# How the second layer's rows reach their experts: blocks stored by token and gathered by an inverted slot table

## The chip, the cores and the metric

The kernel runs on one core of one Trainium2 chip. The metric is the device time of one execution in microseconds (us). Before the change three runs took 1382.59, 1383.05 and 1385.24 us, median 1383.05.

## The reference

```python
def _moe2_ref(x, w_gate, w1, w2):          # x: 1536 tokens x 512, 8 experts, 192 tokens each
    ...
    for idx in order:                      # (token, expert) pairs by falling logit
        tok, e = (int(idx) // E, int(idx) % E)
        if assigned[tok] >= 0 or counts[e] >= cap:
            continue
        assigned[tok] = e
        counts[e] += 1
    ...
    for e in range(E):
        mask = assigned == e
        h = np.maximum(x[mask] @ w1[e], 0.0)
        out[mask] = h @ w2[e]

def reference(**kwargs):
    attn_out = _attn_ref(**attn_kwargs)    # banded attention with 8 global keys
    x = ...                                # 1536 x 512
    x = _moe_ref(x=x, **moe_kwargs)        # first layer: every token through all 8 experts, weighted
    return _moe2_ref(x=x, **moe2_kwargs)   # second layer: every token through one expert
```

## The kernel before, in words

The program runs attention, the dense first layer, and the routed second layer. A Tile scheduler puts the instructions of each engine in an order; `pin` keeps chosen matmuls as they are written, and `tc.issue_after` holds instructions back behind another one on the same engine.

The output of the first layer, `acc` (12 blocks of 128 tokens by 512, one block a column `c`), is the input of the second. Its last products are *held back* (`held_back`, L823 to L843): they run as filler between the steps of the routing, which is seven rounds of proposals and a last one (L1007 to L1087) on small tables. Blocks are finished in the order 8 to 11, 0 to 3, 4 to 7 (`by_time`, L1113); the last four are added by VectorE (L841), the others by ScalarE and GpSimd (L838, L839).

After the rounds twelve small matmuls (L1092, L1094) and three VectorE operations give every token its *slot* `sf` (L1099): expert e has the slots 192e to 192e+191, so a slot says which row of the second layer's input the token becomes. Then:

- `absmax_bound` (L1115, ScalarE) and `pow2_scale` (L1117, helper L98) give one scale `sx2` for all rows. `pow2_scale` reduces over the partitions on GpSimd when the list `on_pool` is filled, otherwise with a matmul by `ident` (L105) and VectorE (L106).
- Twelve indirect stores on GpSimd (L1122) scatter the blocks to the DRAM tensor `xg` by slot. The rows have 513 columns: the last holds the token's number (L1119).
- `load_rows(a)` (L1157) loads the 384 rows of a pair of experts from `xg` with four direct loads on SyncE's queue (L1161 to L1164) into `xr`, three blocks of 128 rows. `turn_rows(a)` (L1168) transposes them on TensorE (L1175), splits them into two f16 parts (L1177, L1178) and copies the token numbers out (L1180).
- For each of four pairs TensorE makes the first product (`mm3`, L710 to L712, by `split_relu` at L1213) and the second (L1224, L1234); `scatter` (L1129, indirect stores on GpSimd at L1130) puts each result at its token's row of `out`.

The second layer's weights lie in DRAM as sixteen `ws` tensors of 2 MB; `fetch` (L1147) loads one into a slot that earlier work has left, from SyncE's queue (L1151). A queue issues in its own order: a load that waits holds back what stands behind it. Before the change the loads of the sixth and seventh weights stand behind the rows of pairs 0 and 1:

```python
    fetch_next(5)
    load_rows(0)
    st = load_rows(1)
    turn_rows(0)
    with tc.issue_after(st.ins):
        fetch_next(2)
```

The slot of the sixth weights held the first layer's W2 of expert 6, which the last held-back product still reads.

Of the kernel before, what the change touches and what calls it, by code (L numbers as in the profile page):

```python
# [20 lines left out]
P = 128  # L21
# [19 lines left out]
def tile_sparse_attention_moe_moe(ctx, tc, q, k, v, ng, nl, wg1, w11, w12, wg2, w21, w22, out, taps=None):  # L41
# [748 lines left out]
        hidden(*x, steps=1)  # L790
    hidden(0, NTB - 1, steps=1)
    done.add(("hidden", 0))
    acc = lat.tile([P, NC, DM + 1], F32, name="acc", tag="acc", bufs=1)
    L = lat.tile([P, NC, E], F32)
    pfs = {}

# [8 lines left out]
    def expert_out(e, tb, steps=0):  # L805
        h = hs.pop((e, tb))
        w, _ = W[e, 1]
        pf = pfs[e]
        for t in range(CPB):
            c = tb * CPB + t  # L810
            ps = mmbank([P, DM], name="py")
            mm3(ps, lambda z, f: h[:, z, f, t * P:t * P + P], lambda z, f: w[:, z, f, :], FC)
            if e == 0:
                latest["dve"] = nc.vector.tensor_scalar(acc[:, c, :DM], ps, pf[:, c:c + 1], None, op0=ALU.mult)
            else:
                latest["dve"] = nc.vector.scalar_tensor_tensor(acc[:, c, :DM], ps, pf[:, c:c + 1], acc[:, c, :DM],  # L816
                                                               op0=ALU.mult, op1=ALU.add)
            if steps:
                pump(steps)
# [3 lines left out]
    def held_back(e, tb, by_pool):  # L823
# [4 lines left out]
        for t in range(CPB):  # L828
            c = tb * CPB + t
            ps = mmbank([P, DM], name="py")  # L830
            for f in range(FC):
                for n, (y1, y2) in enumerate(((0, 0), (0, 1), (1, 0))):
                    pin(nc.tensor.matmul(ps, h[:, y1, f, t * P:t * P + P], w[:, y2, f, :],  # L833
                                         start=f == 0 and n == 0, stop=f == FC - 1 and n == 2))
                if f == FC - 1:
                    if by_pool:
                        y = rawp.tile([P, TB], F32, name="relu", bufs=3)
                        nc.scalar.activation(y[:, :DM], ps, AF.Copy, scale=pf[:, c:c + 1])  # L838
                        nc.gpsimd.tensor_tensor(acc[:, c, :DM], acc[:, c, :DM], y[:, :DM], op=ALU.add)  # L839
                    else:  # L840
                        nc.vector.scalar_tensor_tensor(acc[:, c, :DM], ps, pf[:, c:c + 1], acc[:, c, :DM],  # L841
                                                       op0=ALU.mult, op1=ALU.add)
                yield  # L843

# [9 lines left out]
    def partial_logits(tb):  # L854

        for c in range(tb * CPB, tb * CPB + CPB):
            am = sml.tile([P, 1], F32, name="gam")
            absmax_bound(acc[:, c, :DM], am, rsm)
# [148 lines left out]
    for rnd in range(E - 1):  # L1007
# [76 lines left out]
        nc.vector.tensor_tensor(b, bc_e(tok), bc_c(T[:, 2]), op=ALU.is_gt)  # L1084
        nc.vector.scalar_tensor_tensor(a, b, 1e-37, a, op0=ALU.mult, op1=ALU.is_gt)
        nc.vector.scalar_tensor_tensor(L, a, -1.0e30, L, op0=ALU.mult, op1=ALU.add)
    propose()  # L1087
    run(2)

# [8 lines left out]
    sf = rsm.tile([P, NC], F32, name="sf")  # L1098
    nc.vector.tensor_reduce(sf, sl, axis=AX.X, op=ALU.add)  # L1099
    nc.vector.tensor_scalar(sf, sf, 0.0, float(NT - 1), op0=ALU.max, op1=ALU.min)  # L1100
    si = lcs.tile([P, NC], I32)
    nc.vector.tensor_copy(si, sf)
    finish(held)
    if "slot" in taps:
        nc.sync.dma_start(taps["slot"].rearrange("(c p) -> p c", p=P), si)

    if "x2" in taps:
        for c in range(NC):
            nc.sync.dma_start(taps["x2"][c * P:(c + 1) * P, :], acc[:, c, :DM])


    xam = rsm.tile([P, NC + 1], F32, name="xam")
    by_time = [x for tb in (2, 0, 1) for x in range(tb * CPB, tb * CPB + CPB)]  # L1113
    for c in by_time:
        absmax_bound(acc[:, c, :DM], xam[:, c:c + 1], rsm)  # L1115
    nc.vector.tensor_reduce(xam[:, NC:], xam[:, :NC], axis=AX.X, op=ALU.max)
    sx2 = pow2_scale(xam[:, NC:], "sx2")  # L1117
    xg = drp.tile([NT, DM + 1], F32)
    nc.gpsimd.iota(acc.bitcast(I32)[:, :, DM:], pattern=[[P, NC]], base=0, channel_multiplier=1)  # L1119
    scs = []  # L1120
    for c in by_time:
        st = nc.gpsimd.indirect_dma_start(out=xg, out_offset=bass.IndirectOffsetOnAxis(ap=si[:, c:c + 1], axis=0),  # L1122
                                          in_=acc[:, c, :], in_offset=None)
        for o in scs:
            tc.declare_no_dep(st.ins, o.ins, reason="slots of other tokens")
        scs.append(st)
    outs = []

    def scatter(o, idx):  # L1129
# [38 lines left out]
    def turn_rows(a):  # L1168
        xr = XR.pop(a)
        idx = rsm.tile([P, 3], I32, name="idx", bufs=E // 2)  # L1170
        x2 = xtp.tile([P, 2, KC, 3 * P], F16, name="xt")
        for kc in range(KC):
            pt = aux([P, 3, P], name="px2")
            for z in range(3):
# [92 lines left out]
```

## Time and profile before

| | |
|---|---|
| median of three runs | 1383.05 us |
| the profiled execution's own time | 1383.23 us |
| its span | 1381.4 us |
| TensorE busy | 1305.9 us (95%) |
| VectorE busy | 816.1 us (59%) |
| ScalarE busy | 596.4 us (43%) |
| GpSimd busy | 162.6 us (12%) |

The engines are PE (TensorE), PEld (its weight loads), DVE (VectorE), ACT (ScalarE), POOL (GpSimd) and SP (SyncE, which only issues transfers). The share of busy time is an average over stages with different limits; the second layer fills the last 170 us of the span, and what the change touches lies between about 1207 and 1245 us.

### The profile page before, as it was taken

How to read it: one execution, taken by the hardware profiler on the slowest of the kernel's cores; microseconds unless marked ns; L12 is line 12 of the kernel's file. 1: busy time of each engine (PE TensorE's matmuls, PEld its weight loads, DVE VectorE, ACT ScalarE, POOL GpSimd, SP SyncE). 2: the span in 40 equal slices, each digit the busy share in tenths (PEclk: the TensorE clock that was granted, in tenths of full speed). 3: DMA queues.
4: the chain of work that ended last, by engine and by line, in shares of the span. 5: the costliest groups of instructions: out<-in, count | busy, mean ns of one | idle time of the engine just before them, and what ended most of it. 6: DMA issues, size and time to landing. Idle time of an engine off the chain costs nothing. (4 is left out here: it accounts for less than half of the span.)

```text
span 1381.4 us, 19879 instructions
## 1 busy us (share of the span) xinstructions
PE 1305.9 (95%) x7956; PEld 671.6 (49%) x7956; DVE 816.1 (59%) x1765; ACT 596.4 (43%) x1053; POOL 162.6 (12%) x259
## 2 busy tenths in 40 slices
PE   5899999999999999999999999999988999919998
PEld 3655544444444444444444444455544444407775
DVE  5787586666666666665665654466537878702121
ACT  3667541344253435324341632456534657403332
POOL 5233210000000000000000000010001434030000
PEclk8999999999999999999999999999998999959999
DMA  8352013526433624451462351130010223148740
GB/s 217 82 150 74 1 61 122 183 71 217 140 123 122 217 88 156 149 183 61 147 202 78 117 188 61 51 132 2 1 61 1 104 81 122 62 143 301 274 199 28
DMA packets 96748, 164.93 MB, mean 119 GB/s; under 512 B 50064, under 2 KB 50064, under 8 KB 94096
## 3 DMA queue, kind: packets, MB, share of 16 engines
q1 hardware_dynamic: 94448, 153.18, 33.3%
q0 software_dynamic: 2208, 10.49, 2.0%
q8 instruction: 62, 1.02, 0.3%
q14 instruction: 30, 0.25, 0.1%
HBM read 119.61 MB, written 44.05 MB: 118 GB/s over the span
## 5 line engine op out<-in xcount | busy, mean ns | idle before, releaser
L710 PE MATMUL ph<-xt,wslot 128*128 128x512 f16 x768 | 291.1, 379 | 0.1
L711 PE MATMUL ph<-xt,wslot 128*128 128x512 f16 x768 | 291.0, 379 | 0.0
L712 PE MATMUL ph<-xt,wslot 128*128 128x512 f16 x768 | 291.0, 379 | 0.0
L703 ACT ACTIVATE hslot<-ph 128x512 f16<-128x512 f32 x192 | 114.1, 594 | 253.7 <-PE ph L712 252.0
L710 PE MATMUL py<-wslot,hslot 128*128 128x512 f16 x576 | 218.3, 379 | 0.0
L711 PE MATMUL py<-wslot,hslot 128*128 128x512 f16 x576 | 218.3, 379 | 0.0
L712 PE MATMUL py<-wslot,hslot 128*128 128x512 f16 x576 | 218.3, 379 | 0.0
L705 DVE TENSOR_TENSOR hslot<-relu,hslot 128x512 f16<-128x512 f32 x192 | 132.2, 689 | 111.2 <-ACT relu L704 110.9
L665 DVE TENSOR_REDUCE wam<-raw 128x1 f32<-128x1024 f32 x120 | 143.9, 1212 | 29.8 <-DMA raw<-in_moe_w_dram 29.7
L618 ACT ACTIVATE spill<-raw,s 128x1024 f16<-128x1024 f32 x64 | 72.6, 1146 | 162.7 <-DVE inv L669 64.7
L833 PE MATMUL py<-wslot,hslot 128*128 128x512 f16 x576 | 132.1, 381 | 0.0
L704 ACT ACTIVATE relu<-ph 128x512 f32<-128x512 f32 (+1 forms) x224 | 129.3, 577 | 0.0
L712 PEld LDWEIGHTS <-wslot 128*128 128x128 f16 x768 | 75.1, 98 | 87.4
L710 PEld LDWEIGHTS <-wslot 128*128 128x128 f16 x768 | 75.1, 98 | 86.9 <-issue 2.4
L711 PEld LDWEIGHTS <-wslot 128*128 128x128 f16 x768 | 75.1, 98 | 85.3
L619 DVE SCALAR_TENSOR_TENSOR spill<-raw,s,spill 128x1024 f16<-128x1024 f32 x64 | 81.9, 1283 | 56.5 <-ACT spill L618 55.3
L618 ACT ACTIVATE wslot<-raw,s 128x1024 f16<-128x1024 f32 (+1 forms) x72 | 73.2, 1050 | 76.0 <-DVE s L114 76.0
L816 DVE SCALAR_TENSOR_TENSOR acc<-py,pf,acc 128x512 f32<-128x512 f32 x60 | 45.0, 750 | 84.8 <-PE py L712 84.8
L710 PEld LDWEIGHTS <-hslot 128*128 128x128 f16 x576 | 56.3, 98 | 68.0
L712 PEld LDWEIGHTS <-hslot 128*128 128x128 f16 x576 | 56.3, 98 | 68.0
L711 PEld LDWEIGHTS <-hslot 128*128 128x128 f16 x576 | 56.3, 98 | 67.9
L619 DVE SCALAR_TENSOR_TENSOR wslot<-raw,s,wslot 128x1024 f16<-128x1024 f32 (+1 forms) x72 | 82.8, 1160 | 10.9 <-ACT wslot L618 10.1
(249 smaller groups left out, 1677.3 us busy)
## 6 DMA issues: line engine op xcount, KB each, us to landing
raw<-in_moe_w_dram SPq DMA_DIRECT2D x64, 1024.0 KB, 6.6
ws<-spill SPq DMA_DIRECT2D x64, 512.0 KB, 3.1
w2slot<-ws SPq DMA_DIRECT2D x16, 2048.0 KB, 9.7
hd<-hslot POOLq DMA_DIRECT2D x2, 2048.0 KB, 6.9
hslot<-hd SPq DMA_DIRECT2D x2, 2048.0 KB
qb<-in_q_dram SPq DMA_DIRECT2D x12, 256.0 KB, 3.4
kb<-in_k_dram SPq DMA_DIRECT2D x12, 256.0 KB, 6.7
vo<-in_v_dram SPq DMA_DIRECT2D x12, 256.0 KB, 3.3
```

The lines of the kernel that those rows point to most:

```text
L618: nc.scalar.activation(hi, raw, AF.Copy, scale=s[:, 0:1])
L619: nc.vector.scalar_tensor_tensor(lo, raw, s[:, 0:1], hi, op0=ALU.mult, op1=ALU.subtract)
L665: nc.vector.tensor_reduce(am[:, a:a + 1], part, axis=AX.X, op=ALU.max, apply_absolute_value=True)
L703: nc.scalar.activation(hi, ps, AF.Relu, scale=HS)
L704: latest["act"] = nc.scalar.activation(r[:, :n], ps, AF.Relu, scale=HS)
L705: latest["dve"] = nc.vector.tensor_sub(lo, r[:, :n], hi)
L710: nc.tensor.matmul(out_, lhs(0, a), rhs(0, a), start=a == 0, stop=False)
L711: nc.tensor.matmul(out_, lhs(0, a), rhs(1, a), start=False, stop=False)
L712: nc.tensor.matmul(out_, lhs(1, a), rhs(0, a), start=False, stop=a == n - 1)
L816: latest["dve"] = nc.vector.scalar_tensor_tensor(acc[:, c, :DM], ps, pf[:, c:c + 1], acc[:, c, :DM], op0=ALU.mult, op1=ALU.add)
L833: pin(nc.tensor.matmul(ps, h[:, y1, f, t * P:t * P + P], w[:, y2, f, :], start=f == 0 and n == 0, stop=f == FC - 1 and n == 2))
```

## The change

Blocks are stored to `xg` by token, not by slot, with twelve direct stores on SyncE's queue. The slots are *inverted* on the chip: with slot s = 128a + p of token t, a table `onep` (token by p) and a table `onea` (token by a, holding the token's number where it is 1) are multiplied block by block on TensorE, which leaves at (p, a) the token that has slot 128a + p. That table, `inv`, is the index of three indirect loads a pair on GpSimd, and of the output scatters. The column with the token's number, its copies and the four direct loads a pair go. `on_pool` is emptied ahead of the scale, so its reduction is done by TensorE and VectorE.

```diff
-    acc = lat.tile([P, NC, DM + 1], F32, name="acc", tag="acc", bufs=1)
+    acc = lat.tile([P, NC, DM], F32, name="acc", tag="acc", bufs=1)
...
+    tabs = rawp.tile([P, NT], F32, name="raw", bufs=2)
+    ramp, cols, sq = tabs[:, :P], tabs[:, P:P + NC], tabs[:, 2 * P:2 * P + NC * NC].rearrange("p (c a) -> p c a", a=NC)
+    nc.gpsimd.iota(ramp, pattern=[[1, P]], base=0, channel_multiplier=0, allow_small_or_imprecise_dtypes=True)
+    nc.gpsimd.iota(cols, pattern=[[P, NC]], base=0, channel_multiplier=0, allow_small_or_imprecise_dtypes=True)
     propose()
     run(2)
...
     si = lcs.tile([P, NC], I32)
     nc.vector.tensor_copy(si, sf)
+    nc.vector.tensor_scalar(si, si, P - 1, None, op0=ALU.bitwise_and)
+    sp = rsm.tile([P, NC], F32, name="sp2")
+    nc.vector.tensor_copy(sp, si)
+    onea = tabs.bitcast(F16)[:, NT:NT + NC * NC].rearrange("p (c a) -> p c a", a=NC)
+    onep = rawp.tile([P, NC, P], F16, name="spill", bufs=2)
+    h6 = NC // 2
+    nc.vector.tensor_tensor(onep[:, :h6], sp[:, :h6, None].to_broadcast([P, h6, P]),
+                            ramp[:, None, :].to_broadcast([P, h6, P]), op=ALU.is_equal)
+    nc.gpsimd.tensor_tensor(sf, sf, sp, op=ALU.subtract)
+    nc.vector.tensor_tensor(sq, sf[:, :, None].to_broadcast([P, NC, NC]),
+                            cols[:, None, :].to_broadcast([P, NC, NC]), op=ALU.is_equal)
+    nc.vector.tensor_tensor(onea, sq, tok[:, :, None].to_broadcast([P, NC, NC]), op=ALU.mult)
+    nc.vector.tensor_tensor(onep[:, h6:], sp[:, h6:, None].to_broadcast([P, h6, P]),
+                            ramp[:, None, :].to_broadcast([P, h6, P]), op=ALU.is_equal)
+    run(0)
+    pi = misc([P, NC], name="pinv")
+    for c in range(NC):
+        pin(nc.tensor.matmul(pi, onep[:, c, :], onea[:, c, :], start=c == 0, stop=c == NC - 1))
+    inv = lcs.tile([P, NC], I32)
+    nc.vector.tensor_scalar(inv, pi, 0.0, float(NT - 1), op0=ALU.max, op1=ALU.min)
     finish(held)
...
+    on_pool.clear()
     sx2 = pow2_scale(xam[:, NC:], "sx2")
-    xg = drp.tile([NT, DM + 1], F32)
-    nc.gpsimd.iota(acc.bitcast(I32)[:, :, DM:], pattern=[[P, NC]], base=0, channel_multiplier=1)
-    scs = []
+    xg = drp.tile([NT, DM], F32)
     for c in by_time:
-        st = nc.gpsimd.indirect_dma_start(out=xg, out_offset=bass.IndirectOffsetOnAxis(ap=si[:, c:c + 1], axis=0),
-                                          in_=acc[:, c, :], in_offset=None)
...
+        nc.sync.dma_start(xg[c * P:c * P + P, :], acc[:, c, :])
...
-        xr = rawp.tile([P, 3, DM + 1], F32, name="raw", bufs=2)
-        r0, r1 = 2 * a * CAP, (2 * a + 1) * CAP
-        nc.sync.dma_start(xr[:, 0, :], xg[r0:r0 + P, :])
-        nc.sync.dma_start(xr[0:RM, 1, :], xg[r0 + P:r0 + CAP, :])
-        nc.sync.dma_start(xr[64:64 + RM, 1, :], xg[r1 + P:r1 + CAP, :])
-        st = nc.sync.dma_start(xr[:, 2, :], xg[r1:r1 + P, :])
+        xr = rawp.tile([P, 3, DM], F32, name="raw", bufs=2)
+        for z in range(3):
+            st = nc.gpsimd.indirect_dma_start(out=xr[:, z, :], out_offset=None, in_=xg,
+                                              in_offset=bass.IndirectOffsetOnAxis(ap=inv[:, 3 * a + z:3 * a + z + 1],
+                                                                                  axis=0))
...
-        nc.vector.tensor_copy(idx, xr.bitcast(I32)[:, :, DM])
-        X2[a] = x2, idx
+        X2[a] = x2, inv[:, 3 * a:3 * a + 3]
```

Where the instructions come to stand is decided by the scheduler. The first place is VectorE behind the sum of the slots. The rows with a + are new, those with a - are of before; L841 is the last block's accumulation.

```order
+L1104 TENSOR_SCALAR sf<-sf 128x12
+L1107 CAST si<-sf 128x12
+L1108 TENSOR_SCALAR si<-si 128x12
+L1110 CAST sp_11066<-si 128x12
+L1114 TENSOR_TENSOR spill<-sp_11066,raw 128x768
+L1117 TENSOR_TENSOR raw<-sf,raw 128x144
+L1120 TENSOR_TENSOR spill<-sp_11066,raw 128x768
+L1119 TENSOR_TENSOR raw<-raw,tok 128x144
+L1127 TENSOR_SCALAR inv<-pinv 128x12
 L841 SCALAR_TENSOR_TENSOR acc<-py,pf,acc 128x512
-L1100 TENSOR_SCALAR sf<-sf 128x12
-L1102 CAST si<-sf 128x12
```

The last accumulation stood ahead of the slots' last two operations and now stands behind the whole inversion. At the same place TensorE now has, between the slots' matmul (L1098) and the scale's (L105), the twelve pairs of L1125 ahead of the last three pairs of L833; before, the L833 pairs followed L1094 directly.

```order
L1098 LDWEIGHTS before
L1098 MATMUL pk<-Bz,before 128x96
L1125 LDWEIGHTS spill [waits DVE_49]
L1125 MATMUL pinv<-raw,spill 128x12 [waits PE_49]
...
L833 LDWEIGHTS hslot
L833 MATMUL py<-wslot,hslot 128x512
...
L105 MATMUL bc<-ident,xam 128x128 [waits DVE_49]
```

So the last held-back product, which the accumulation L841 and the slot of the sixth weights wait for, ends behind matmuls that wait for VectorE.

The second place is SyncE's queue, now, from the second of the second layer's weights on (`ws_1_3898` is the sixth, `ws_0_4070` the seventh; L1143 are the stores).

```order
L1168 DMA w2slot<-ws_1_2559 128x8192
L1143 DMA xg<-acc 128x512 x3
L1168 DMA w2slot<-ws_0_3078 128x8192
L1143 DMA xg<-acc 128x512
L1168 DMA w2slot<-ws_1_3225 128x8192
L1143 DMA xg<-acc 128x512 x3
L1168 DMA w2slot<-ws_0_3413 128x8192
L1143 DMA xg<-acc 128x512 x4
L1168 DMA w2slot<-ws_1_3898 128x8192
L1143 DMA xg<-acc 128x512
L1168 DMA w2slot<-ws_0_4070 128x8192
```

Before, it was:

```order
L1151 DMA w2slot<-ws_0_3413 128x8192
L1161 DMA raw<-xg 128x513
L1162 DMA raw<-xg 64x513
L1163 DMA raw<-xg 64x513
L1164 DMA raw<-xg 128x513
...
L1151 DMA w2slot<-ws_1_3898 128x8192
L1151 DMA w2slot<-ws_0_4070 128x8192
```

The sixth weights stood behind the rows of two pairs; now they stand ahead of the last store, and the seventh directly behind it.

The third place is GpSimd from the last slots to the end.

```order
-L1122 DMA xg<-acc,si 1536x513
-L102 ISA
-L102 ISA amax<-xam 128x1
-L1122 DMA xg<-acc,si 1536x513 x11
-L1130 DMA out_dram<-spill,idx 1536x512 x12
-L1260 UNCONDITIONAL_BRANCH
+L1116 TENSOR_TENSOR sf<-sf,sp_11066 128x12
+L1178 DMA raw<-xg,inv 128x512 x12
+L1147 DMA out_dram<-spill,inv 1536x512 x12
```

Twelve scatters with a reduction among them became twelve gathers, and all twelve stand ahead of the first output scatter.

## Rows read from the trace of the kernel before

**Rows 1.** Head of the page.
```profile
span 1381.4 us, 19879 instructions
```
**Rows 2.** Busy time by stretches: us, each engine (count), granted clock, DMA share, GB/s.
```profile
1238.80:1244.30 5.50, 4.73 (x23) 3.59 (x24) 1.94 (x5) 2.10 (x4) 0.00 (x0) 0.50 0.99 327
1244.30:1300.00 55.70, 55.52 (x523) 43.32 (x521) 14.25 (x28) 21.18 (x45) 2.87 (x3) 1.00 0.87 333
```
**Rows 3.** Timeline at the slots' end: start, us, engine, line, operation, [idle before <-releaser].
```profile
1207.81 0.81 PE L833 MATMUL py<-wslot,hslot 128*128 128x512 f16 x3
...
1208.60 0.25 DVE L1099 TENSOR_REDUCE sf<-sl 128x12 f32<-128x96 f32 x1
1208.77 0.74 DVE L841 SCALAR_TENSOR_TENSOR acc<-py,pf,acc 128x512 f32<-128x512 f32 x1
...
1209.62 0.17 DVE L1102 CAST si<-sf 128x12 int32<-128x12 f32 x1
```
**Rows 4.** Timeline of GpSimd from 1210 to 1232 us.
```profile
1210.10 1.20 POOL L1122 DMA_INDIRECT xg<-acc,si  x1 [24.55 <-DVE si L1102]
...
1217.95 0.38 POOL L102 PARTITION_ALL_REDUCE amax<-xam  x1 [6.65 <-issue]
...
1218.52 1.20 POOL L1122 DMA_INDIRECT xg<-acc,si  x1 [0.20 <-issue]
...
1220.02 0.96 POOL L1122 DMA_INDIRECT xg<-acc,si  x1 [0.30 <-issue]
...
1231.40 0.96 POOL L1122 DMA_INDIRECT xg<-acc,si  x1 [0.30 <-issue]
```
**Rows 5.** Timeline at the restart of TensorE.
```profile
1238.86 0.90 PE L1175 MATMUL px<-ident,raw 128*128 128x128 f32 x3 [30.24 <-DMA raw<-xg]
...
1240.92 0.17 DVE L1180 COPY idx<-raw 128x3 int32<-128x3 int32 x1 [21.89 <-DMA raw<-xg]
...
1241.99 0.80 PE L710 MATMUL ph<-xt,w2slot 128*128 128x192 f16 x4 [0.24 <-ACT xt L1177]
```
**Rows 6.** VectorE's prices: timeline (1181, 1247 us), and the page's costliest groups.
```profile
1180.87 0.17 DVE L1079 TENSOR_SCALAR rtau<-prs 128x8 f32<-128x8 f32 x1 [0.85 <-PE prs L1075]
1181.07 0.16 DVE L1080 TENSOR_TENSOR rtau<-rtau,prs 128x8 f32<-128x8 f32 x1
...
1247.47 0.56 DVE L705 TENSOR_TENSOR xt<-relu,xt 128x384 f16<-128x384 f32 x1 [2.58 <-ACT relu L704]
...
L705 DVE TENSOR_TENSOR hslot<-relu,hslot 128x512 f16<-128x512 f32 x192 | 132.2, 689 | 111.2 <-ACT relu L704 110.9
```
**Rows 7.** Timeline: an addition on GpSimd, and twelve small matmuls.
```profile
1143.22 7.21 POOL L839 TENSOR_TENSOR acc<-acc,relu 128x512 f32<-128x512 f32 x1 [3.98 <-ACT relu L838]
...
1178.10 0.64 PE L1065 MATMUL prc<-comb,spill 128*128 128x8 f16 x12
```
**Rows 8.** SyncE's queue: landing after 1181.45, the issues, landings after 1259.5 and 1262.55, one stretch.
```profile
w2slot<-ws SPq DMA_DIRECT2D x1, 2048.0 KB, 8.8
...
1251.67 8.24 SPq L1151 DMA_DIRECT2D w2slot<-ws  x2
...
w2slot<-ws SPq DMA_DIRECT2D x1, 2048.0 KB, 10.6
...
1262.59 0.99 SPq L1162 DMA_DIRECT2D raw<-xg  x1
...
raw<-xg SPq DMA_DIRECT2D x1, 128.2 KB, 8.6
...
1131.00:1133.00 2.00, 2.00 (x22) 1.08 (x20) 0.70 (x3) 0.44 (x1) 0.00 (x0) 1.00 0.99 426
```
**Rows 9.** Output scatters' landings after 1376 and 1278.5 us, and weight loads' issue.
```profile
out_dram<-spill,idx POOLq DMA_INDIRECT x1, 2.7
...
1276.80 0.80 SPq L1151 DMA_DIRECT2D w2slot<-ws  x2
...
out_dram<-spill,idx POOLq DMA_INDIRECT x1, 8.2
```

More of the change, by code (lines that the diff above doesn't have):

```diff
@@ L813, in expert_out @@
             if e == 0:
-                latest["dve"] = nc.vector.tensor_scalar(acc[:, c, :DM], ps, pf[:, c:c + 1], None, op0=ALU.mult)
+                latest["dve"] = nc.vector.tensor_scalar(acc[:, c, :], ps, pf[:, c:c + 1], None, op0=ALU.mult)
             else:
-                latest["dve"] = nc.vector.scalar_tensor_tensor(acc[:, c, :DM], ps, pf[:, c:c + 1], acc[:, c, :DM],
+                latest["dve"] = nc.vector.scalar_tensor_tensor(acc[:, c, :], ps, pf[:, c:c + 1], acc[:, c, :],
                                                                op0=ALU.mult, op1=ALU.add)
@@ L838, in held_back @@
                         nc.scalar.activation(y[:, :DM], ps, AF.Copy, scale=pf[:, c:c + 1])
-                        nc.gpsimd.tensor_tensor(acc[:, c, :DM], acc[:, c, :DM], y[:, :DM], op=ALU.add)
+                        nc.gpsimd.tensor_tensor(acc[:, c, :], acc[:, c, :], y[:, :DM], op=ALU.add)
                     else:
-                        nc.vector.scalar_tensor_tensor(acc[:, c, :DM], ps, pf[:, c:c + 1], acc[:, c, :DM],
+                        nc.vector.scalar_tensor_tensor(acc[:, c, :], ps, pf[:, c:c + 1], acc[:, c, :],
                                                        op0=ALU.mult, op1=ALU.add)
@@ L857, in partial_logits @@
             am = sml.tile([P, 1], F32, name="gam")
-            absmax_bound(acc[:, c, :DM], am, rsm)
+            absmax_bound(acc[:, c, :], am, rsm)
             s = pow2_scale(am, "sp", bufs=2)
@@ L1102, in tile_sparse_attention_moe_moe @@
     nc.vector.tensor_copy(si, sf)
+    nc.vector.tensor_scalar(si, si, P - 1, None, op0=ALU.bitwise_and)
[18 more added lines that the diff above has]
+    nc.vector.tensor_scalar(inv, pi, 0.0, float(NT - 1), op0=ALU.max, op1=ALU.min)
     finish(held)
-    if "slot" in taps:
-        nc.sync.dma_start(taps["slot"].rearrange("(c p) -> p c", p=P), si)
     if "x2" in taps:
         for c in range(NC):
-            nc.sync.dma_start(taps["x2"][c * P:(c + 1) * P, :], acc[:, c, :DM])
+            nc.sync.dma_start(taps["x2"][c * P:(c + 1) * P, :], acc[:, c, :])
     xam = rsm.tile([P, NC + 1], F32, name="xam")
@@ L1114, in tile_sparse_attention_moe_moe @@
     for c in by_time:
-        absmax_bound(acc[:, c, :DM], xam[:, c:c + 1], rsm)
+        absmax_bound(acc[:, c, :], xam[:, c:c + 1], rsm)
     nc.vector.tensor_reduce(xam[:, NC:], xam[:, :NC], axis=AX.X, op=ALU.max)
+    on_pool.clear()
     sx2 = pow2_scale(xam[:, NC:], "sx2")
-    xg = drp.tile([NT, DM + 1], F32)
-    nc.gpsimd.iota(acc.bitcast(I32)[:, :, DM:], pattern=[[P, NC]], base=0, channel_multiplier=1)
-    scs = []
+    xg = drp.tile([NT, DM], F32)
     for c in by_time:
-        st = nc.gpsimd.indirect_dma_start(out=xg, out_offset=bass.IndirectOffsetOnAxis(ap=si[:, c:c + 1], axis=0),
-                                          in_=acc[:, c, :], in_offset=None)
-        for o in scs:
-            tc.declare_no_dep(st.ins, o.ins, reason="slots of other tokens")
-        scs.append(st)
+        nc.sync.dma_start(xg[c * P:c * P + P, :], acc[:, c, :])
     outs = []
@@ L1169, in turn_rows @@
         xr = XR.pop(a)
-        idx = rsm.tile([P, 3], I32, name="idx", bufs=E // 2)
         x2 = xtp.tile([P, 2, KC, 3 * P], F16, name="xt")
```

## The prediction

> **What bounds the kernel now.** I read the page first: the profiled execution spans 1381.4 us [rows 1] and took 1383.23 us, 1.8 us around the span and 0.18 above the median of the three runs (1383.05), so the sum below is made against 1383.23. Then TensorE's busy time by stretches [rows 2]: from 1244.3 on it is busy 55.5 of 55.7 us, so the second layer is bound by TensorE once it runs. Ahead of it lies a hole: the first transpose at 1238.86 had TensorE idle for 30.24 us, released by the loads of the rows [rows 5]. What the change can win lies there, and the timeline shows what fills it [rows 3 to 5]. The slots are ready at 1209.79 (cast at 1209.62, 0.17 long). The first scatter starts at 1210.10, then GpSimd sits 6.65 us before the reduction for the scale, and eleven scatters follow, one about every 1.27 us, the last starting at 1231.40. Only when all have landed may the rows be loaded back. The copy of the token numbers, which reads all three blocks of the pair, is released at 1240.92, so that is when the pair's last rows are there. The first product starts at 1241.99.
>
> **The sum: when do the last rows of pair 0 land after the change?** Everything behind that moment is TensorE's own work and moves with it.
>
> 1. *Slots to one-hot tables (VectorE).* The sum of slots ends at 1208.85 (1208.60 + 0.25) [rows 3]. Four operations on 12 columns follow each other; two such stand 0.20 us apart [rows 6]: 0.8, to 1209.65. Two compares of 768 elements come next: TENSOR_TENSOR takes 0.56 for 384 and 0.689 for 512 [rows 6], so 0.129 for each 128 more, and 0.95 for 768 (an estimate; the low end is 0.69, the 512 row itself, the high end twice 0.95 if the broadcast operands slow it). Two operations on 144 elements by the same slope take 0.32. Together 2.54, to 1212.2. GpSimd's subtraction of 12 columns runs beside the first compare.
> 2. *Inversion (TensorE).* Twelve matmuls of 12 columns: the twelve of 8 columns took 0.64 at most [rows 7], to 1212.8. The new order puts the last three matmuls of the held-back product behind these; they took 0.81 [rows 3], to 1213.6. The conversion to whole numbers is 0.17 beside them.
> 3. *Last block of x2.* VectorE's accumulation (0.74) [rows 3] therefore ends at 1214.4 and no longer at 1209.51. This is what the inversion costs: 4.9 us.
> 4. *Its store.* In SyncE's queue the last store stands behind a load of 2 MB second-layer weights, whose slot is released by those same three matmuls. So the load leaves at 1213.6 and the store at 1214.5. A load of that size issued at 1181.51 alone landed after 8.8 us [rows 8]: 1222.4. What happens to a small transfer behind a large one also has a row: the second weight load of the 1251.67 piece starts at 1259.59 (the piece's end less one issue of 0.32) and landed 10.6 later, at 1270.2; the 128 KB of L1162 issued behind it at 1262.59 landed 8.6 later, at 1271.2, 1.0 us after it [rows 8]. So the store lands at 1223.4. The other eleven stores are issued as their blocks are done, under TensorE's work, and cost nothing; the cover is that work, and without it each would be one transfer of 256 KB. The weights queued behind them are wanted only after the first product of pair 0.
> 5. *Gathers (GpSimd).* The first starts 0.3 after its last wait, as the first scatter did (1209.79 to 1210.10) [rows 3, 4]: 1223.7. Scatter starts stand 1.50 and then 1.27 apart [rows 4]; the trace has no gather, but it is the same instruction with the direction turned, so the third starts at 1226.5.
> 6. *Landing.* No row shows a gather's. Its low end is a scatter of the same size with nothing beside it, 2.7; its high end one beside two weight loads, 8.2 [rows 9]. I take 4.0, nearer the low end: the weight load queued behind the last store moves 2.1 MB at the 426 GB/s of such a load's middle [rows 8], 4.9 us, so it has most of its data across when the third gather starts, even counted from the store's landing. The last rows land at 1230.5, against 1240.9: **10.4 us earlier**.
>
> Nothing of this comes back later. The scale is not waited for: its reduction ended 8.8 us after the last accumulation (1209.51 to 1218.33), with the 6.65 us in it [rows 3, 4], and 1214.4 + 8.8 is still before 1230.5. The nine gathers of the other pairs stand ahead of the first output scatter in GpSimd's queue; the last three wait for the transposes of pair 1, which come with the end of pair 0's first product, and take 3.8 us, while the first output follows a whole second product later. The removed loads and copies of token numbers were off the path. 1383.23 - 10.4 = **1372.8 us**.
>
> *TensorE's clock.* It was granted 0.50 (1.2 GHz) for the first 5.5 us after the hole and 1.00 (2.4 GHz) after [rows 2]. The new hole is shorter but still over ten us, so I leave the restart as it was. Bounds: those 5.5 us at the full level would give back at most 2.7; transposes that come one block at a time could keep it low 2.8 us longer, which costs 1.4. With the compares (0.5 less to 1.9 more) and the landing (2.7 to 5.3 alone) the forecast's own range is 1370 to 1376.
>
> **The rivals.**
>
> *A: the store overtakes.* If the last store does not wait behind the 2 MB load, it lands 2.7 after 1214.5, at 1217.2, and the third gather starts at 1220.3. Beside two weight loads it lands after 4.0 to 8.2, at 1224.3 to 1228.5: 12.4 to 16.6 us won, 1366.6 to 1370.8. Against it stands L1162's 8.6 us [rows 8]; for it, that this was a load behind a load and not a store.
>
> *B: the gathers are held by the weights.* In the old order the row loads stood ahead of the next weights in one queue; now two weight loads go first and the gathers come from another queue. If the second of them is still streaming, the row is 8.2 us beside loads (two issued from 1276.80, the scatter at 1278.54) against 2.7 alone [rows 9]: the third gather lands at 1234.7, 6.2 us are won, **1377.0**. Against it: by my sum the load's data ends about when the gathers start. The Trainium skill, "DMA: Bandwidth & Descriptors", section "Issuing engines are not separate DMA queues", speaks for this rival: DMAs run on the same 16 engines and interleave whichever engine started them, so issuing the rows from GpSimd gets them past nothing. By that rule, the trace agrees: 8.2 against 2.7 us. The same page's section "Queues, rings and completion order" says that an engine goes round-robin between queues packet by packet, which would cost a 256 KB gather about its own data time again, an estimate of 0.6 us at the page's 436 GB/s; the row of 8.2 is far above that, and the row decides.
>
> *C: the index chain is slow.* GpSimd's subtraction stands between VectorE's operations. An addition on GpSimd beside a busy VectorE took 7.21 us [rows 7]. If this one does too, it outlasts the compare's 0.95 by 6.3 and the gain shrinks to 4.1, 1379.1; with B as well it is no change. Against it: VectorE then waits for it and is no longer in its way.
>
> *D, slower: gathers that don't spread.* The sum lets a gather move its rows over all 16 engines. The scatters did: eleven of 263 KB started within the 12.9 us from 1218.52 to 1231.40 [rows 4], 224 GB/s, or 14 for each engine. If the three gathers of a pair ran through one engine, 786 KB at 14 GB/s are 56 us: rows at 1280 in place of 1240.9, at least 39 us slower, **1422**. It decides from the point at which the third lands after 1240.9, 14.4 us after its start, or under 54 GB/s for the three. Nothing in the trace speaks for it except that it holds no gather.
>
> *E: the change doesn't take effect,* because something other than rows releases the first transposes. The row at 1238.86 names the loads, so I give it next to nothing.
>
> **How the numbers follow.** Forecast 0.57, A 0.13, B 0.19, C 0.06 (half of it within 2.8 us of before), D 0.04, E 0.01. 0.2% is 2.8 us, about what a measurement of this kernel can tell from no change. Faster by more: forecast, A, B and half of C, 0.92, of which I keep 0.91. Within it: half of C and E, rounded to 0.05. Slower: 0.04. The time is the forecast's, 1372.8. The range reaches from the upper part of A (1367.5) over B with a little more (1378.0), and leaves out the lower part of A, C and D.
>
> **What would show it.** Right: GpSimd has no reduction and no 6.65 us wait after 1208; the last store is issued near 1214.5 and the first gather near 1223.7; the first transposes start near 1228 and the first product near 1231.6, with the clock at 0.50 for some 5 us; behind that TensorE is busy without gaps. Wrong: a first gather near 1218 (A); a third gather that takes over 6 us to land while a weight load streams (B); VectorE waiting for GpSimd between the compares (C); gathers that take over 14 us each (D); gaps on TensorE after the restart that end with a transfer.

## The result and the profile after

The changed kernel took 1372.8 us (median; 1371.69 to 1373.88), the kernel before 1384.07 us beside it: ratio 0.9919, 95% interval 0.9902 to 0.9936, some 9 to 13.5 us faster. The profiled execution took 1372.69 us. The forecast was 1372.8.

Where the time went is read best from one point that both kernels pass: the start of the last product that counts places for the slots (`pk`, L1094 before, L1098 after). It stood at 1207.77 before and at 1208.25 after; this start differs by up to 3.7 us between executions of the kernels below, so differences are taken from it and called the **lag**. The first product of the second layer came 34.22 us behind it before (1241.99 [rows 5]) and 23.25 us after. From the same point to the span's end it is 173.63 us before (1381.4 [rows 1]) and 162.65 after: 10.98 us won, of which the lag has 10.97. Nothing was won or lost elsewhere.

The head of the page after:

```profile
span 1370.9 us, 19908 instructions
```

The timeline of VectorE, GpSimd, TensorE and SyncE's queue after, from the slots to the first product (start, length, engine, line, operation, [idle before <- what ended it]; it answers to [rows 3 to 5]):

```profile
1208.25 0.20 PE L1098 MATMUL pk<-Bz,before 128*128 128x96 bf16 x1
1209.08 0.25 DVE L1103 TENSOR_REDUCE sf<-sl 128x12 f32<-128x96 f32 x1
...
1210.20 0.96 DVE L1114 TENSOR_TENSOR spill<-sp,raw 128x768 f16<-128x768 f32 x1
1210.24 0.98 POOL L1116 TENSOR_TENSOR sf<-sf,sp 128x12 f32<-128x12 f32 x1 [24.22 <-DVE sp L1110]
...
1212.35 0.30 DVE L1119 TENSOR_TENSOR raw<-raw,tok 128x144 f16<-128x144 f32 x1
1212.71 0.46 PE L1125 MATMUL pinv<-raw,spill 128*128 128x12 f16 x12 [4.26 <-DVE raw L1119]
1213.03 1.11 PE L833 MATMUL py<-wslot,hslot 128*128 128x512 f16 x3
...
1214.17 0.32 SPq L1168 DMA_DIRECT2D w2slot<-ws  x1
1214.18 0.75 DVE L841 SCALAR_TENSOR_TENSOR acc<-py,pf,acc 128x512 f32<-128x512 f32 x1 [0.80 <-PE py L833]
1214.96 0.32 SPq L1143 DMA_DIRECT2D xg<-acc  x1
...
1217.29 0.22 DVE L1155 TENSOR_SCALAR f<-f,sx 128x8 f32<-128x8 f32 x1
...
1223.84 1.19 POOL L1178 DMA_INDIRECT raw<-xg,inv  x1 [12.61 <-issue]
1225.33 0.95 POOL L1178 DMA_INDIRECT raw<-xg,inv  x1 [0.30 <-issue]
1226.58 0.95 POOL L1178 DMA_INDIRECT raw<-xg,inv  x1 [0.30 <-issue]
...
1228.33 1.70 PE L1190 MATMUL px<-ident,raw 128*128 128x128 f32 x6 [11.85 <-DMA raw<-xg,inv]
1230.36 0.90 PE L1190 MATMUL px<-ident,raw 128*128 128x128 f32 x3 [0.33 <-DMA raw<-xg,inv]
1231.50 0.80 PE L710 MATMUL ph<-xt,w2slot 128*128 128x192 f16 x4 [0.24 <-ACT xt L1192]
```

The reader is to see three waits in a row. VectorE and TensorE make the index until 1213.4, and the last block of x2 is held back behind that (L833 at 1213.03; before, it stood at 1207.81 [rows 3]). The store leaves at 1214.96, behind a load of weights. Then nothing happens on GpSimd until 1223.84: the profile writes "issue" there, since it sees no releaser, but the scale was ready at 1217.5 and the index at 1213.4, so only the store is left to wait for, 8.9 us after its issue (experiments 3 and 4 bear this out). The third gather starts at 1226.58 and its transposes at 1230.36, 3.8 us later.

Busy time by stretches after (us, each engine's busy time (count), granted clock, DMA share, GB/s; it answers to [rows 2]):

```profile
1228.30:1231.50 3.20, 2.60 (x10) 1.64 (x10) 0.02 (x1) 0.63 (x2) 2.38 (x3) 0.50 0.74 210
1231.50:1233.90 2.40, 2.40 (x14) 2.03 (x14) 1.84 (x4) 1.47 (x3) 0.57 (x1) 0.51 0.53 172
1233.90:1289.60 55.70, 55.52 (x523) 43.24 (x522) 13.84 (x25) 21.31 (x45) 8.09 (x9) 1.00 0.70 268
```

The restart is that of before, moved: 2.4 us after the first product the granted clock goes from 0.50 (1.2 GHz) to 1.00 (2.4 GHz), and TensorE is then busy 55.52 of 55.7 us, to the hundredth what [rows 2] has.

### The profile page after: what moved, and what is told of

It reads as the page before. It is cut to its first block, busy times and chain, and to the rows that moved or that the text cites. A ratio compares the mean times of both kernels' runs of the same rounds, so it can differ in the third digit from the quotient of the medians.

```text
span 1370.9 us, 19908 instructions
## 1 busy us (share of the span) xinstructions
PE 1308.3 (95%) x7969; PEld 672.8 (49%) x7969; DVE 819.8 (60%) x1769; ACT 596.5 (44%) x1053; POOL 166.9 (12%) x260
## 4 chain that ended last, share of the span: by engine, by line
PE 78%; issue 10%; DVE 7%; POOL 3%; DMA 1%; ACT 1%; POOLq 0%; SPq 0%; DVEq 0%; ACTq 0%
PE ph L710 12%; PE ph L712 12%; PE ph L711 12%; PE py L710 9%; PE py L712 9%; PE py L711 9%; PE py L833 4%; PE pa L510 2%; PE pe L491 1%; DVE xt L1045 1%; PE ps L465 1%; POOL ex L481 1%; DVE xt L1043 1%; PE pg L138 1%; DVE xt L1046 1%
## 5 line engine op out<-in xcount | busy, mean ns | idle before, releaser
L833 PE MATMUL py<-wslot,hslot 128*128 128x512 f16 x576 | 132.3, 381 | 0.0
L102 POOL PARTITION_ALL_REDUCE amax<-wam x30 | 10.6, 353 | 661.3 <-DVE wam L666 661.3
```

## The experiments

The theory was that of the prediction: the time is set by slots, inversion, last block, store behind a 2 MB load, gathers. All times stand beside the kernel before, run between them (medians 1384.07 to 1385.12 us). The last three columns come from the one profiled execution of each kernel.

| run | time, us | ratio to before, 95% | lag, us | full clock after first product, us | to the end, us |
|---|---|---|---|---|---|
| before | 1384.07 | | 34.22 | 2.5 | 173.63 |
| after | 1372.8 | 0.9919 (0.9902 to 0.9936) | 23.25 | 2.4 | 162.65 |
| after again | 1372.0 | 0.9904 (0.9885 to 0.9922) | 23.57 | 2.1 | 162.86 |
| 1: scale alone | 1376.38 | 0.9947 (0.9931 to 0.9964) | 27.74 | 2.1 | 166.96 |
| 2: scale back on GpSimd | 1374.44 | 0.9926 (0.9909 to 0.9942) | 22.66 | 3.4 | 162.58 |
| 3: store first | 1371.96 | 0.9909 (0.9892 to 0.9926) | 22.67 | 3.2 | 162.44 |
| 4: weights last | 1367.05 | 0.9876 (0.9859 to 0.9892) | 17.66 | 4.2 | 158.00 |
| 5: product first | 1368.55 | 0.9878 (0.9860 to 0.9895) | 18.58 | 3.9 | 158.61 |
| 6: both 4 and 5 | 1364.55 | 0.9849 (0.9831 to 0.9866) | 14.01 | 4.8 | 154.61 |
| 7: other queue | 1374.99 (one run) | | 25.75 | 3.3 | 165.47 |
| 7 again | 1375.95 | 0.9943 (0.9927 to 0.9960) | 25.37 | 3.9 | 165.31 |
| 8: other queue, one load | 1372.41 | 0.9912 (0.9895 to 0.9929) | 23.36 | 5.5 | 164.08 |
| 9: store first, 2 KB pieces | 1371.79 | 0.9905 (0.9888 to 0.9921) | 21.86 | 3.9 | 161.97 |
| 10: other queue, 2 KB pieces | 1372.95 | 0.9914 (0.9896 to 0.9933) | 22.55 | 3.3 | 162.24 |

"To the end" is the span less the start of the last `pk` product. "Full clock" is the start of the first product of the second layer that takes 0.25 us in place of 0.37, less the start of the first product.

### The scale's reduction (1 and 2)

Experiment 1 is the kernel before with one line of the change: the scale's maximum over the partitions goes to TensorE and VectorE.

```diff
+    on_pool.clear()
     sx2 = pow2_scale(xam[:, NC:], "sx2")
```

> The kernel before, with the change's smallest part alone: the scale is reduced by TensorE and VectorE and no longer on GpSimd between the scatters. Theory (the hole is a chain on GpSimd, and its 6.65 us idle piece before the reduction lies on it): the second scatter starts about 1.5 us after the first, near 1211.6 and not at 1218.52, everything behind moves 6.9 us forward, 1376.3 us; so two thirds of the change's gain come from this one line. Rival (the piece is covered, the scatters are paced by their transfers and the gain belongs to the gathers): within 1 us of before.

Measured: 1376.38 us. GpSimd's timeline in experiment 1:

```profile
1208.77 1.20 POOL L1123 DMA_INDIRECT xg<-acc,si  x1 [24.55 <-DVE si L1102]
1210.27 0.96 POOL L1123 DMA_INDIRECT xg<-acc,si  x1 [0.30 <-issue]
...
1222.91 0.96 POOL L1123 DMA_INDIRECT xg<-acc,si  x1 [0.30 <-issue]
```

The first and second scatter stand 1.50 apart where they stood 8.42 apart (1210.10 and 1218.52 [rows 4]); the last starts 14.14 after the first and no longer 21.30. The lag falls from 34.22 to 27.74. So **6.5 of the 11 us of the change belong to this line**, and 4.5 to stores by token and gathers together. The medians would give the line more, 8.3 of 11.3 us, but its profiled execution reached the last `pk` product 1.33 us earlier than that of before, ahead of all that the line touches.

Experiment 2 is the changed kernel without that line.

```diff
-    on_pool.clear()
     sx2 = pow2_scale(xam[:, NC:], "sx2")
```

> The changed kernel with the scale's reduction put back on GpSimd. Theory (GpSimd only waits for the last store at that time): the reduction and the 6.65 us before it end by 1223.5, the first gather still starts near 1223.8, time as after the change, 1372.8 within 1. Rival (the 6.65 us stand in the way as they did between the scatters): the first gather starts 5 us later or more, 1378 or above.

GpSimd's timeline in experiment 2:

```profile
1218.90 0.38 POOL L102 PARTITION_ALL_REDUCE amax<-xam  x1 [5.81 <-issue]
1225.39 1.19 POOL L1177 DMA_INDIRECT raw<-xg,inv  x1 [6.12 <-issue]
```

The reduction comes back, with 5.81 us of idle ahead of it, and costs nothing: it is over at 1219.28, and the gather waits until 1225.39 for the store that left at 1216.52, 8.9 us as in the changed kernel. The lag is 22.66, not longer than 23.25. The time is 1.6 us higher than that of the change, though the two ratios to before can't be told apart (0.9926 and 0.9919, with intervals that overlap); in the profiled executions it lies ahead of the reduction, since this one reached the last `pk` product at 1210.12 and took 162.58 from there to the end, against 162.65. The line is worth 6.5 us in the old order, where GpSimd is the path, and nothing in the new one, where a transfer is.

### The store and the weights (3 and 4)

Experiment 3 issues the two loads of weights behind the last store.

```diff
-        nc.sync.dma_start(xg[c * P:c * P + P, :], acc[:, c, :])
+        last = nc.sync.dma_start(xg[c * P:c * P + P, :], acc[:, c, :])
...
-    st = load_rows(1)
+    load_rows(1)
...
-    with tc.issue_after(st.ins):
+    with tc.issue_after(last.ins):
         fetch_next(2)
```

> The changed kernel with the sixth and seventh weights' loads held behind the last store in SyncE's queue. Theory (the last store lands 8.5 us after its issue because it stands behind 2 MB in the queue): it lands 2 to 3.1 us after its issue at 1215, the first gather starts near 1218.3 (5.5 earlier), the third near 1221; but now both weight loads stream beside the gathers, which land after 4.4 to 8.2 us, so the first product starts between 1226.5 and 1230.4 and the time is 1368 to 1372. Rival (the store shares the engines with the weights whatever the order): it lands near 1222 as before, time within 1.5 of 1372.8.

Measured: 1371.96 us. The timeline in experiment 3, and under it the DMA issues of the first three gathers there (count, median us from issue to landing):

```profile
1213.89 0.32 SPq L1143 DMA_DIRECT2D xg<-acc  x1
1214.30 0.89 SPq L1168 DMA_DIRECT2D w2slot<-ws  x2
...
1217.06 1.19 POOL L1178 DMA_INDIRECT raw<-xg,inv  x1 [6.74 <-DVE f L1155]
...
1225.80 0.90 PE L1190 MATMUL px<-ident,raw 128*128 128x128 f32 x3 [10.39 <-DMA raw<-xg,inv]
1228.25 1.54 PE L1190 MATMUL px<-ident,raw 128*128 128x128 f32 x6 [1.55 <-DMA raw<-xg,inv]
```

```profile
raw<-xg,inv POOLq DMA_INDIRECT x3, 9.0
```

The first gather follows the store's issue by 3.2 us in place of 8.9. (The profile names VectorE's `f` as what released it, as it does in experiment 4; `f` is the operation that ended last, at 1216.43, and not what is waited for: in experiment 6 the first gather starts at 1215.40 and `f` at 1215.90.) But both loads now stream beside the gathers, and these land after 9.0 us in place of 3.7. What is won on one transfer is given back on the next: rival B of the prediction, made real by this edit.

Experiment 4 holds the loads until the third gathered block of pair 0 has landed: a transfer of 64 bytes that reads that block goes ahead of them in the queue.

```diff
-    st = load_rows(1)
+    load_rows(1)
+    d = nc.sync.dma_start(drp.tile([1, 16], F32, name="scr"), XR[0][0:1, 2, 0:16])
     turn_rows(0)
-    with tc.issue_after(st.ins):
+    with tc.issue_after(d.ins):
         fetch_next(2)
```

> The changed kernel with the two weight loads held, by a transfer of 64 bytes that reads the third block of pair 0, until that block has landed. Theory: the store lands 2 to 3.1 us after 1215, gathers start near 1218.3, the third lands 3.7 us or less after 1221, the first product starts near 1225.7, 5.8 earlier than after the change: 1367.0. The weights are issued near 1225 and are wanted only in pair 1. Rival (the weights come too late from there): TensorE shows gaps that end with a transfer and the gain is eaten, 1372 or above.

The timeline of SyncE's queue, GpSimd and TensorE in experiment 4:

```profile
1214.12 0.32 SPq L1143 DMA_DIRECT2D xg<-acc  x1
1223.58 0.25 SPq L1208 DMA_DIRECT2D scr<-raw  x1
1223.93 0.80 SPq L1168 DMA_DIRECT2D w2slot<-ws  x2
...
1217.21 1.19 POOL L1178 DMA_INDIRECT raw<-xg,inv  x1 [7.14 <-DVE f L1155]
...
1223.61 0.90 PE L1190 MATMUL px<-ident,raw 128*128 128x128 f32 x3 [0.61 <-DMA raw<-xg,inv]
1224.76 0.80 PE L710 MATMUL ph<-xt,w2slot 128*128 128x192 f16 x4 [0.24 <-ACT xt L1192]
```

1367.05 us, expected 1367.0. The timeline shows the first gather 3.1 us behind the store's issue and the third block's transposes 3.7 us behind its gather's start (1219.95), and no product later waits for a load, though the weights leave some 10 us later than in the changed kernel. The lag is 17.66: the weights ahead of the last rows cost the change 5.6 us.

### The held-back product (5 and 6)

Experiment 5 puts the last products of the first layer ahead of the twelve of the inversion, as in the kernel before.

```diff
-        run(0)
+        finish(held)
...
-    finish(held)
```

> The changed kernel with the last three matmuls of the held-back product placed ahead of the inversion's twelve. Theory (the inversion costs 4.9 us because the last block, the weights' slot and with them the last store wait for it): the weights leave near 1209.3, the store near 1210.4 and lands near 1218.7, the first gather starts near 1219.0, 4.8 earlier; 1368.0. Rival (the index is what the gathers wait for, so the inversion is on the path wherever the product stands): first gather within 1 us of 1223.8, time within 1.5 of 1372.8.

Measured: 1368.55 us, 0.5 above the 1368.0 expected. The store leaves 1.76 us behind the last `pk` product (1209.65 and 1207.89), where it left 6.71 behind it: 4.95 us sooner. The lag is 18.58, 4.67 less.

Experiment 6 makes both edits, 4 and 5.

> Product ahead of the inversion and the two weight loads held behind pair 0's rows, together. Theory: the last store leaves near 1210.4 and lands near 1213, the index is ready near 1214, so now the index is what the gathers wait for; the first starts near 1214.4, the third near 1217.2 and lands near 1220.9; the first product starts near 1222, 9.5 earlier than after the change: 1363.3. Rival (the two gains overlap, both being the wait for the last store): no better than the better of the two alone, 1367.

The timeline of experiment 6:

```profile
1210.65 0.32 SPq L1142 DMA_DIRECT2D xg<-acc  x1
...
1215.40 1.19 POOL L1177 DMA_INDIRECT raw<-xg,inv  x1 [3.01 <-DVE inv L1127]
...
1222.90 0.80 PE L710 MATMUL ph<-xt,w2slot 128*128 128x192 f16 x4 [0.24 <-ACT xt L1191]
```

1364.55 us is the best of all kernels here, ratio 0.9849 to before, and some 8 us under the change. The first gather is now released by the index (`inv`), no longer by a transfer: store and weights are off the path, the inversion is on it. (It starts 0.85 us behind the end of `inv` at 1214.55, where the prediction's step 5 had put 0.3; why is open.) Most of the 1.25 us above the expected 1363.3 lies in the clock. Stretches of experiment 6:

```profile
1222.90:1227.70 4.80, 4.80 (x29) 4.32 (x29) 2.27 (x4) 1.48 (x3) 2.35 (x3) 0.50 1.00 387
1227.70:1283.40 55.70, 55.52 (x513) 42.57 (x512) 13.42 (x24) 21.49 (x45) 7.07 (x8) 1.00 0.80 319
```

Behind the first product TensorE runs at 0.50 for 4.8 us here, and for 2.4 after. Half of the 2.4 us between them is lost work: 1.2 us. Why it rose later is not settled. Here the transposes come block by block with TensorE idle between them, which the prediction had named as a cause; but in experiment 5 they run together as in the changed kernel (six, then three), and the clock came after 3.9 us all the same, while in 7 and 10 they come block by block and it came after 3.3. The price itself is seen in the table: from the change to experiment 4 the lag falls by 5.59 and the clock comes 1.8 us later, so 5.59 less 0.9 is 4.7, and the column to the end has 4.65; for 5 it is 4.67 less 0.75, 3.9, against 4.04; for 6, 9.24 less 1.2, 8.0, against 8.04.

### Another queue, and the size of the pieces (7 to 10)

Experiment 7 leaves the loads alone and issues the last store from ScalarE's queue.

```diff
-        nc.sync.dma_start(xg[c * P:c * P + P, :], acc[:, c, :])
+        (nc.scalar if c == 2 * CPB - 1 else nc.sync).dma_start(xg[c * P:c * P + P, :], acc[:, c, :])
```

> The changed kernel with only the last store issued from ScalarE's queue, the weights ahead of it in SyncE's as they are. Theory (order within the queue holds the store): on a queue of its own it is issued near 1215 and lands earlier than 8.5 us after, between the 2 to 3 us of a store alone and the 8.2 us of a transfer beside two loads; the first gather starts between 1218.5 and 1223. Rival (only the shared engines count): first gather near 1223.8, as after the change.

Measured: 1374.99 us in one run, a miss for theory and rival alike. The store was issued at 1214.59, both loads from 1213.69, and the first gather started at 1225.85: 11.3 us behind the store, later than behind a load in its own queue. Experiment 7 was therefore run again, timed, beside a variant (8) that keeps the store on ScalarE's queue but holds the second load as in experiment 4.

> The same kernel as the single run with the last store on ScalarE's queue and both loads on SyncE's, now timed. If the late first gather (11 us after the store's issue) belongs to the kernel and not to that execution, the lag from the start of the first gate-rank product to the first product is 25 to 26 us again and the time 1374 to 1375; if it was that execution alone, the lag is 23 to 23.5 and the time about 1372.

> Last store of rows on ScalarE's queue as in the run before, but only the sixth load of weights beside it; the seventh is held until the third gathered block of pair 0 has landed. Open: why the store alone on its queue landed about 11 us after its issue, against some 8.5 behind one load on SyncE's queue. Theory S: the store gets a share of the 16 engines beside each load on them, so with one load it takes about twice the 3.1 us that it took alone: 5.5 to 6.5 us, first gather 6 to 7 us after the issue (near 1221), first product near 1228, 20 to 21 us after the start of the first gate-rank product; about 1369.5 us. Theory L: it lands when the data that was on the engines ahead of it has, whichever queue: about 8 us, as behind the load on SyncE's queue; first gather near 1223.5, first product near 1231, 23 to 23.5 us after that start; about 1372.

```diff
+    d = nc.sync.dma_start(drp.tile([1, 16], F32, name="scr"), XR[0][0:1, 2, 0:16])
     turn_rows(0)
     with tc.issue_after(st.ins):
-        fetch_next(2)
+        fetch_next(1)
+    with tc.issue_after(d.ins):
+        fetch_next(1)
```

The repeat came out as the first: 1375.95 us, lag 25.37, the store issued at 1214.41 and the first gather at 1225.49, 11.1 us. With one load (8) it is 8.8 us (1214.03 to 1222.79): theory L by its numbers, an equal share (S) is out. How the two queues moved shows in the packets, the pieces in which the profile counts what a queue moves. Queues of the repeat, first from 1214 to 1218 and then from 1218 to 1224 (q1 is SyncE's, q10 ScalarE's; packets, MB, share of 16 engines):

```profile
q1 hardware_dynamic: 74, 1.21, 92.2%
...
q1 hardware_dynamic: 157, 2.31, 89.9%
q10 hardware_dynamic: 141, 0.26, 11.3%
```

For 3.6 us after its issue the store moves nothing. Then its packets go about one for one with those of the loads, 141 beside 157, but a packet of a load holds 16 KB (1.21 MB in 74) and one of the store 2 KB, so the store has a tenth of the bytes. The Trainium skill, "DMA: Bandwidth & Descriptors", section "Queues, rings and completion order", says that an engine takes turns between its queues packet by packet. By that rule, these rows agree, if a packet of the profile is one of the page's: the two queues move 157 and 141. The prediction took from it that a small transfer beside a large one costs about its own data time again; these rows, with packets of unlike size, don't bear that out.

If this is right, smaller packets of the load must help. Experiments 9 and 10 are 3 and 7 with these two loads written as eight transfers each, 2 KB for a partition.

```diff
-        nc.sync.dma_start(t, spilled[e, which])
+        if m in (5, 6):
+            for y in range(2):
+                for q in range(0, WE, 1024):
+                    nc.sync.dma_start(t[:, y, q:q + 1024], spilled[e, which][:, y, q:q + 1024])
+        else:
+            nc.sync.dma_start(t, spilled[e, which])
```

> The kernel with the last store ahead of both loads of weights, and those two loads written as eight transfers of 256 KB each, in pieces of 2 KB for a partition in place of 16 KB. Theory, packet for packet: with 16 KB packets each 2 KB packet of a gather waited for one packet of the load (in the run with whole loads 23 packets of gathers moved beside 21 of the loads from 1223 to 1224, with 0.09 MB against 0.34), so packets of equal size leave the gathers half of the bytes: they land after 3.5 to 4.5 us in place of 7.8, the first product comes 18.5 to 19.5 us after the start of the first gate-rank product in place of 22.7, and the time is about 1368.5 us. Rival, bytes: what counts is the data queued on the engines, not the size of its packets; the gathers land after 7 to 8 us, the lag is 22.5 to 23, the time about 1372.

> The kernel with the last store on ScalarE's queue beside both loads, these written in pieces of 2 KB as in the run before. Theory, packet for packet: the store lands 5 to 7 us after its issue in place of 11 (it got none of its packets moved for some 4 us, then shares evenly: 0.26 MB at half of 426 GB/s is 1.2 us), the first gather starts about 5 us earlier relative to the start of the first gate-rank product than with whole loads, and the first product comes 19 to 21.5 us after that start in place of 25.7; about 1369 to 1371 us. Rival, bytes: as with whole loads, 25 to 26 us and about 1375.

Queues of experiment 10 from 1218 to 1219:

```profile
q1 hardware_dynamic: 118, 0.23, 61.0%
q10 hardware_dynamic: 94, 0.17, 44.7%
```

Queues from 1223 to 1224, of experiment 3 (q0 carries the gathers):

```profile
q1 hardware_dynamic: 21, 0.34, 80.2%
q0 software_dynamic: 23, 0.09, 22.9%
```

and of experiment 9:

```profile
q1 hardware_dynamic: 81, 0.16, 51.8%
q0 software_dynamic: 53, 0.18, 49.6%
```

For the store the theory holds in its numbers: in experiment 10 it has 0.17 MB in a microsecond beside 0.23 of the load, and the first gather starts 5.5 us after its issue (1215.11 to 1220.60) in place of 11.1; the rival's 25 to 26 us of lag are out there. The first product is only 2.8 us sooner than in 7 (lag 22.55, expected 19 to 21.5), because the gathers, early now, run beside the rest of the loads. For the gathers (9) the share turned as foretold, 0.18 MB beside 0.16 in place of 0.09 beside 0.34, but the landing did not follow: the transposes of the first block start 6.6 us after its gather (8.7 in experiment 3), those of the third 8.0 (8.5), against 3.5 to 4.5 expected. The lag of 21.86 lies below the rival's 22.5 to 23 and far above the theory's. So shares go by packets and their size, as the queue rows show; that isn't the whole landing. Nor do 9 and 10 test the size alone: SyncE needs 10.0 and 9.1 us to issue the sixteen pieces where the two loads took 0.8 to 0.9, so fewer bytes are queued when the small transfer comes. How much of the store's gain in 10 is owed to that, no run separates. What holds the first packets back is open: in experiments 3 and 9 alike the gather issued at 1217.1 to 1217.2 moved none before 1221.

### The change once more

> The changed kernel itself, for a comparison on the same chip: 1372.8 within 1.5.

1372.0 us, lag 23.57, the first gather at 1223.14 and the first product at 1230.81: the first run's picture.

## Why the prediction was right

**Steps 1 and 2, slots and inversion.** The tables were done at 1212.65, expected 1212.2. The whole stage stood 0.48 later in this execution, which is all of that difference; the compares took 0.96 and 0.95 where the slope gave 0.95: the broadcast operands cost nothing. GpSimd's subtraction took 0.98 and outlasted the compare beside it by 0.06. The twelve matmuls took 0.46, the bound was 0.64.

**Step 3, the last block.** Expected end 1214.4, measured 1214.93. The three products were put at 0.81, from a row at a granted clock of 1.00, and took 1.11: they now stand behind TensorE's wait of 4.26 us for the tables, and the clock fell while they ran (1.00 from 1212.7 to 1213.2, 0.50 from 1213.7 to 1214.2). In experiments 5 and 6, which put them ahead of that wait, they took 0.81. That this order costs 4.9 us is shown by experiment 5: the store leaves 4.95 us sooner without it.

**Step 4, the store.** Load 1214.17 and store 1214.96, expected 1213.6 and 1214.5; the store landed 8.6 us after its issue (the gather's start less the prediction's 0.3), expected 8.9. Taking the price of a small transfer behind a large one from L1162 [rows 8] was the step on which most hung. Experiments 3 and 4 show what it is without the load ahead: the gather starts 3.1 to 3.2 us after the store's issue, 8.9 in the changed kernel.

**Step 5, the gathers.** First and third at 1223.84 and 1226.58, expected 1223.7 and 1226.5. The spacing of scatters [rows 4] held for gathers.

**Step 6, the landing.** 3.7 us by the median of the three, expected 4.0. The argument behind it, that the second load has most of its data across when the third gather starts, holds. Queues after, first from 1225 to 1226, then from 1226 to 1227 and from 1227 to 1228:

```profile
q1 hardware_dynamic: 28, 0.46, 106.9%
...
q0 software_dynamic: 47, 0.18, 44.8%
q1 hardware_dynamic: 22, 0.11, 27.6%
...
q0 software_dynamic: 66, 0.21, 78.5%
q1 hardware_dynamic: 1, 0.00, 0.1%
```

The load has the engines until 1226 and is through before 1228, and the gathers take over. With the loads held back the first three gathers of experiment 4 took 3.5 by their median; with both loads beside them those of experiment 3 took 9.0, above the high end of 8.2.

**The clock** restarted as before, 2.4 us after the first product. A later rise, for which the prediction kept up to 1.4 us, did not come here; in the experiments it cost 0.9 us (4), 1.2 (6) and, by the same working, 1.5 (8).

**The cover.** That the scale was not waited for held even with the reduction on GpSimd (experiment 2). No later product waited for a transfer.

**The rivals.** A (store overtakes) did not happen, and experiment 7 shows that even a queue of its own does not bring it. B (gathers held by the weights) is a true mechanism, of about the size given (9.0 us against 8.2), but in the changed kernel the store behind the first load is itself what keeps the gathers out of the loads' way; experiment 3 turns it on. C (slow subtraction) is out by 0.98 us against 7.21 [rows 7]. D (gathers that don't spread) is out: landings of 3.7 us for 256 KB. E is out.

**Luck and bounds.** That the forecast hits the measured time to the tenth is luck. The changed kernel won 10.98 us where 10.4 was forecast, with the store and the gather each landing 0.3 sooner than put, and its profiled execution reached the last `pk` product 0.48 later, which hid the difference. The range of 1370 to 1376 for the forecast alone is narrower than its own terms make when they fall together (1368.3 to 1377.4), and the 5.3 us that it gives as the landing's upper bound "alone" stand in no row.

What the prediction did not say is that its 10.4 us have two sources. Against the old order without the hole (experiment 1, lag 27.74) the direct stores and gathers win only 4.5 us, because the order of the products costs 4.7 and the weights ahead of the last rows 5.6. Without both (experiment 6) they win 13.7; the three terms would make 14.8, but the index takes over as what the gathers wait for.

## What to carry to other kernels

When a chain of small steps is replaced, write down the new chain with each queue it stands in: here the last store's place behind one load of 2 MB cost more (8.9 us in place of 3.2) than the inversion's ahead of the last block (4.7), and moving it past the load gave the time back on the next transfer until the loads were held as well. Try the cheapest part of a change alone: one line of this one held 6.5 of 11 us. Count a restart of TensorE from where its clock comes back, not from its first instruction.

## What was not expected of the hardware

- A store on a queue of its own beside two loads of 2 MB was followed by its first gather later (11.1 and 11.3 us after the issue) than one in the loads' queue behind the first of them (8.9): once the store moved, packets went about one for one, and those of the loads were eight times as large.
- Beside such loads a small transfer is late to move its first packet. The store moved none in 3.6 us in experiment 7, none in 3.8 in 8, with one load alone, and none in 2.1 in 10, with pieces of 2 KB; with nothing ahead of it, in 3 and 4, its first packet came within 0.9 us. The gathers of 3 and 9 moved none in some 4 us, whether the loads came in 16 or 2 KB; with nothing beside it the gather of experiment 4 issued at 1217.21 moved its first between 1219 and 1220. The cause was not found.
- GpSimd stands idle for 5.81 us ahead of the reduction over the partitions in experiment 2, for 6.65 before [rows 4], with no wait that the profile shows. A change of GpSimd's configuration is issued where the idle starts; these are the rows for it of the reduction's line, before and in experiment 2 (length in ns, first and last start in us):

```profile
L102 POOLq MODIFY_POOL_CONFIG  x2: 37/37/37, 1211.6 to 1211.6; - x2
...
L102 POOLq MODIFY_POOL_CONFIG  x2: 5/5/5, 1213.3 to 1213.3; - x2
```

  The 44 earlier reductions of this line have no such instruction. That the change of configuration fills these microseconds fits the rows, but no run tests it.
- The full clock came 2.1 to 5.5 us after the first product, in kernels whose restart holds the same instructions; half of the difference is lost work. Whether the blocks reach TensorE one by one doesn't decide: so they do in experiments 4, 6 and 8 (4.2, 4.8 and 5.5), but also in 7 and 10 (3.3), and experiment 5, with its first two together, had 3.9. What decides was not found.
- TensorE's granted clock fell from 1.00 to 0.50 shortly behind a wait of some 4.3 us, for the tables of the index, so three products that take 0.81 us took 0.94 (experiment 3) to 1.43 (4). In 2, in the same order, they took 0.81.
